# Other priorities for the early steps and fixed engines for normalising, copies and casts in an attention and MLP kernel

## The chip, the core and the metric

The kernel runs on one core of a Trainium2 chip. The metric is the device time of one execution in microseconds (us). TensorE is called PE, VectorE DVE, ScalarE ACT, GpSimd POOL, and SyncE SP, which issues all the transfers (DMA) of this kernel.

## What is computed

For each of 8 batches and 8 heads (576 positions of width 64) two softmax attentions are added: one over positions pooled by four, repeated four times, and a local one over the seven nearest positions. The sum, 4608 rows of 512, goes through a maxout MLP. Weights and products are held to float32 accuracy or better. The core of the reference:

```python
q_d = q.reshape(B, H, Sd, factor, D).mean(axis=3)       # k_d, v_d likewise
out_d = sm_attn(q_d, k_d, v_d)
out_up = np.repeat(out_d, factor, axis=2)
mask = np.abs(pos[:, None] - pos[None, :]) < factor      # seven neighbours
scores = np.where(mask, scale * np.matmul(q, k.transpose(0, 1, 3, 2)), -1e9)
attn_out = out_up + np.matmul(softmax(scores), v)        # x: 4608 x 512
h = np.maximum(np.maximum(x @ w1, x @ w2), x @ w3)       # 512 -> 768, three times
return h @ w_out                                         # 768 -> 512
```

## The kernel before

**Tiling.** The MLP runs in 9 blocks of 512 rows. A block j has 288 matmuls of 128x512 on PE: 6 column groups (`ft`) times 3 weights times 12 for the first layer (`mlp_in`), and 72 for the second (`mlp_out`). Twelve, not four, because each operand is a sum of two reduced-precision parts: `xhi`/`xlo` for the rows, `whi`/`wlo` for the weights, `hhi`/`hlo` for the hidden layer, `wohi`/`wolo` for the last weight; a product takes hi·hi, hi·lo and lo·hi. In PSUM `pm` has three banks: a group of 12 fills `ph_j_ft_i`; ACT copies the first to `t`, DVE takes the maximum with the second and the third (`t<-pm,t`), ACT casts to `hhi` (`hh_0r<-t`) and DVE subtracts for `hlo` (`hh_1r<-t,hh_0r`). A bank is free when its reader is done.

**Weights.** They arrive as words of 64 bit. For each of 6 column groups `weight_in(ft)` loads `rawin_ft`, and `weight_split` turns it into `whi`, `wlo`: ACT takes an absolute value, DVE runs two one-operand passes (TENSOR_SCALAR on `pvb`), two bit passes (SCALAR_TENSOR_TENSOR), ACT casts to `whi`, DVE subtracts for `wlo`. `weight_out` does the same with the last weight in six smaller pieces. In the trace `rawin_0` and `rawin_1` are `hh`, the later ones `wo`, the last weight's pieces `pvb`. Matmuls on `ft` need `whi` and `wlo` of that `ft`, and those on a row group c (0 to 3) need `xhi_j_c` and `xlo_j_c`.

**Attention.** Index n = 0..16 is half a block: four heads. The halves n = 0 to 3 (blocks 0 and 1) take a dense form in `dense(j, plan)`: steps listed in `PLAN`, each with a priority; `q` loads q and k, `qk` adds them up by four (`hp`, then `qkT`), `s0`/`s1` (`band_scores`) make local scores on PE, their maxima on DVE, exponentials (70 columns each) on ACT, the sum's reciprocal on DVE and the normalising product either as one DVE instruction or as eight on ACT; `v0`/`v1` (`band_values`) transpose them, copy them to SBUF (`ptb`), multiply with v and add the pooled part into `xb` (`t<-pm,od`, `x<-pa,od`); `sums`, `pv` do the pooled part (`pd`, `pt`, `od`). For n = 1 some of the tiles stand in the buffers of late weights, so `hp` reads `whi` and `wlo` in the trace. The halves n from 4 go through DRAM scratch and run beside the MLP of earlier blocks (`begin`, `attention`). `transposes(j, c)` casts to `xhi` and subtracts for `xlo`.

**What sets the order.** Every instruction is first recorded. `Recorder.place` then puts them in order, engine by engine, with a list of prices: it takes whatever can start first, and among those that can start, the lowest priority; an operation with several forms goes to the engine that would end first, plus a bias (`TO_ACT`, `MUL_BIAS`). Assumed delays are added between engines: `LAG`, and `CARE` for n from 4. `BEGIN` is the priority of the first steps of n = 4, `WLOAD`, `WMAKE`, `WOUT` those of the weights; `COLD_US` is how long PE is priced at half speed. The result is a fixed order on each engine (L492 issues it all), and each engine works strictly through its own list.

Of the kernel before, what the change touches and what calls it, by code (L numbers as in the profile page):

```python
# [32 lines left out]
VBUFS = 3  # L33
LAG = 200.0
TAGS = ('pm', 'pm', 'pa', 'pa')
WLOAD = (110.0, 165.0, 190.0, 320.0, 255.0, 350.0)
WMAKE = (150.0, 120.0, 110.0, 255.0, 285.0, 390.0)
WOUT = 300.0
PLAN = (
    (  # L40
        ("q", 0, -120.0),
        ("v", 0, -120.0),
        ("qk", 0, 0.0),
        ("s0", 0, -40.0),
        ("s1", 0, 100.0),
        ("tail", 0, 0.0),
        ("q", 1, 110.0),
        ("v", 1, 110.0),
        ("sums", 0, -40.0),
        ("vd", 0, 0.0),  # L50
        ("qk", 1, 70.0),
        ("s0", 1, 80.0),
        ("s1", 1, 100.0),
        ("tail", 1, 130.0),
        ("pv", 0, 180.0),
        ("v0", 0, -50.0),
        ("v1", 0, 60.0),
        ("sums", 1, 50.0),
        ("vd", 1, 220.0),
        ("pv", 1, 100.0),  # L60
        ("v0", 1, 70.0),
        ("v1", 1, 150.0),
    ),
    (
        ("q", 0, 200.0),
        ("v", 0, 200.0),
        ("qk", 0, 170.0),
        ("s0", 0, 320.0),
        ("s1", 0, 200.0),
        ("tail", 0, 270.0),  # L70
        ("sums", 0, 200.0),
        ("vd", 0, 200.0),
        ("pv", 0, 200.0),
        ("v0", 0, 200.0),
        ("v1", 0, 80.0),
        ("q", 1, 330.0),
        ("v", 1, 330.0),
        ("qk", 1, 420.0),
        ("s0", 1, 240.0),
        ("s1", 1, 360.0),  # L80
        ("tail", 1, 300.0),
        ("sums", 1, 240.0),
        ("vd", 1, 390.0),
        ("pv", 1, 300.0),
        ("v0", 1, 240.0),
        ("v1", 1, 300.0),
    ),
)
CARE = {'near': (2000.0, 2000.0, 1.1500000000000001), 'far': (3000.0, 2000.0, 1.2)}
NEAR = 8  # L90
# [99 lines left out]
class Recorder:  # L190
# [46 lines left out]
    def add(self, forms, bias={}):  # L237
# [4 lines left out]
        for method, args, kw in next(iter(forms.values())):  # L242
# [7 lines left out]
            ins += r  # L250
        o.prio = self.prio
        if "PE" in forms and o.prio >= 0.0:
# [257 lines left out]
def local_global_attention_maxout_kernel(ctx: ExitStack, tc: tile.TileContext, qk_d, qke_d, vw_d, vt_d, wi_d, wo_d, v, ident_d, mask_d, diag_d, band_d, out):  # L510
# [14 lines left out]
    def at(prio, lag=0.0, care=None):  # L525
# [18 lines left out]

    def copy(dst, src, engines=("ACT", "DVE"), bias={}):
        forms = {"ACT": [("copy", (dst, src), {})], "DVE": [("tensor_copy", (dst, src), {})]}
        return rec.add({e: forms[e] for e in engines}, bias)

# [144 lines left out]
    def pooled_scores(n):  # L693
# [24 lines left out]
        if n in DENSE:  # L718
# [6 lines left out]
            with together():  # L725
# [27 lines left out]
    def pooled_values(n):  # L753
# [123 lines left out]
    def band_scores(n, pr, tag):  # L877
# [19 lines left out]
        one = [("tensor_tensor", (), dict(out=sm, in0=sm, in1=z.unsqueeze(3).broadcast_to([P, 2, FAC, KWIN]), op=ALU.mult))]  # L897
        rec.add({"DVE": one, "ACT": muls}, TO_ACT)
        state[n]["sm", pr] = sm

    def band_values(n, pr, tag):
# [6 lines left out]
        for i in range(2):  # L908
# [48 lines left out]
    def transposes(j, c):  # L957
# [5 lines left out]
        else:  # L963
# [58 lines left out]
    def attention(n):  # L1022
# [92 lines left out]
```

## Time and profile before

| | |
|---|---|
| time before, median of 3 runs | 721.51 us (720.29 to 724.8) |
| the profiled execution: time | 722.12 us |
| its span, first to last instruction | 720.3 us |
| mean granted clock of PE | 0.985 |
| PE busy | 687.6 us (95%) |
| DVE busy | 525.8 us (73%) |
| ACT busy | 405.0 us (56%) |
| POOL busy | 204.3 us (28%) |

How it is read: a busy share is the time in which the engine ran instructions; idle time is named after whatever released the engine. All instructions have the line L492, so groups are told apart by engine, operation, tile names and shapes. Two full-speed matmuls of 128x512 start 0.2275 us apart; their own durations of 0.39 us overlap.

### The profile page before, as it was taken

The page shows a single profiled execution, that of the slowest core. Times are in us where ns is not written, and L with a number is a line of the kernel's source. Part 1 is how long each engine was busy: PE and PEld are TensorE (multiplying, and loading weights), DVE is VectorE, ACT ScalarE, POOL GpSimd, SP SyncE. Part 2 cuts the span into 40 slices and gives each one's busy share as a digit, 9 for nine tenths or more (in the row PEclk, how much of TensorE's full clock was granted, in tenths as well). Part 3 has the DMA queues.
Part 4 walks back from the last instruction along what each step waited for, and adds up shares of the span by engine and source line. Part 5 has one row for each costly group of instructions (what it writes and reads, how often), then busy time and mean ns, then how long its engine had stood idle before and what let it go on. Part 6 is the DMA issues. An engine that isn't in the chain of part 4 may idle for free.

```text
span 720.3 us, 13541 instructions
## 1 busy us (share of the span) xinstructions
PE 687.6 (95%) x4756; PEld 556.6 (77%) x4756; DVE 525.8 (73%) x928; ACT 405.0 (56%) x1437; POOL 204.3 (28%) x269
## 2 busy tenths in 40 slices
PE   3589999899999999999999999999999999999996
PEld 2467787688888888888887888888888788888885
DVE  5699998877878796879878987797868788531220
ACT  4988686473928482847475639273836577221111
POOL 0023200051615450445055307070515345000000
PEclk9959999999999999999999999999999999999999
DMA  9944234667486758493995574747475772210002
GB/s 275 416 173 154 88 124 149 160 157 153 121 189 186 124 131 179 110 201 75 235 208 114 102 204 120 181 92 210 115 189 109 177 133 70 55 59 30 0 1 58
DMA packets 190817, 101.35 MB, mean 141 GB/s; under 512 B 161454, under 2 KB 166605, under 8 KB 189981
## 3 DMA queue, kind: packets, MB, share of 16 engines
q1 hardware_dynamic: 190749, 100.49, 55.7%
q8 instruction: 37, 0.61, 0.4%
q14 instruction: 31, 0.25, 0.1%
HBM read 71.23 MB, written 29.23 MB: 139 GB/s over the span
## 4 chain that ended last, share of the span: by engine, by line
PE 85%; DVE 6%; ACT 4%; DMA 4%; issue 0%; SPq 0%; ACTq 0%; DVEq 0%
PE pm L492 78%; PE pa L492 7%; DVE pvb L492 1%; DMA pvb<-in_wo_dram 1%; ACT sm L492 1%; DMA wo<-in_wi_dram 1%; DVE wo L492 1%; DMA whi<-in_qk_dram 1%; DMA qk<-in_qk_dram 1%; ACT whi L492 1%; ACT pvb L492 1%; DVE t L492 1%; DVE hp L492 0%; DVE hh L492 0%; DVE wlo_0r L492 0%; ACT whi_0r L492 0%
## 5 line engine op out<-in xcount | busy, mean ns | idle before, releaser
L492 PE MATMUL pm<-xhi_0r,whi_0r 128*128 128x512 f32 x648 | 253.8, 392 | 0.9 <-ACT xhi_0r L492 0.9
L492 PE MATMUL pm<-xhi_0r,wlo_0r 128*128 128x512 f32 x648 | 253.2, 391 | 0.0
L492 PE MATMUL pm<-xlo_0r,whi_0r 128*128 128x512 f32 x648 | 253.2, 391 | 0.0
L492 POOL TENSOR_TENSOR pvb<-v,s 128x256 f32<-128x256 f32 x216 | 166.1, 801 | 171.2 <-DVE s L492 99.4
L492 ACT ACTIVATE pvb<-v,s 128x64 f32<-128x64 f32 x704 | 176.3, 343 | 26.0 <-DVE s L492 14.8
L492 PEld LDWEIGHTS pm<-xhi_0r,whi_0r 128*128 128x128 f32 x648 | 121.7, 188 | 27.9 <-ACT xhi_0r L492 1.3
L492 PEld LDWEIGHTS pm<-xhi_0r,wlo_0r 128*128 128x128 f32 x648 | 121.6, 188 | 25.8 <-issue 0.6
L492 PEld LDWEIGHTS pm<-xlo_0r,whi_0r 128*128 128x128 f32 x648 | 121.7, 188 | 25.6 <-issue 0.8
L492 DVE TENSOR_TENSOR t<-pm,t 128x512 f32<-128x512 f32 x108 | 73.8, 683 | 74.2 <-PE pm L492 69.1
L492 DVE TENSOR_TENSOR pvb<-pvb 128x768 f32<-128x768 f32 x112 | 109.6, 979 | 12.2 <-POOL pvb L492 7.6
L492 PE MATMUL pm<-wo_0r,hh_0r 128*128 128x512 f32 x216 | 84.4, 393 | 2.0 <-ACT wo_0r L492 2.0
L492 ACT CAST hh_0r<-t 128x512 fp32r<-128x512 f32 x54 | 33.5, 620 | 92.5 <-DVE t L492 92.2
L492 PE MATMUL pm<-wo_0r,hh_1r 128*128 128x512 f32 x216 | 84.5, 392 | 0.0
L492 PE MATMUL pm<-wo_1r,hh_0r 128*128 128x512 f32 x216 | 84.4, 391 | 0.0
L492 ACT CAST xhi_0r<-t 128x512 fp32r<-128x512 f32 x32 | 19.8, 620 | 61.6 <-DVE t L492 58.6
L492 PEld LDWEIGHTS pm<-wo_0r,hh_0r 128*128 128x128 f32 x216 | 40.5, 188 | 11.9 <-ACT wo_0r L492 2.5
L492 POOL TENSOR_TENSOR hv<-v 128x128 f32<-128x128 f32 (+1 forms) x14 | 12.8, 924 | 124.0 <-DMA v<-in_v_dram 111.8
L492 PEld LDWEIGHTS pm<-wo_1r,hh_0r 128*128 128x128 f32 x216 | 40.6, 188 | 8.8 <-issue 0.2
L492 PEld LDWEIGHTS pm<-wo_0r,hh_1r 128*128 128x128 f32 x216 | 40.5, 188 | 8.6 <-issue 0.2
L492 ACT COPY t<-pm 128x512 f32<-128x512 f32 x54 | 31.5, 584 | 27.7 <-PE pm L492 27.6
L492 DVE TENSOR_TENSOR hh_1r<-t,hh_0r 128x512 fp32r<-128x512 f32 x54 | 39.6, 733 | 9.9 <-ACT hh_0r L492 9.6
L492 ACT ACTIVATE pd<-pa,nz 128x144 f32<-128x144 f32 x90 | 33.1, 383 | 14.1 <-issue 11.1
(134 smaller groups left out, 711.2 us busy)
## 6 DMA issues: line engine op xcount, KB each, us to landing
v<-in_v_dram SPq DMA_DIRECT2D x55, 320.0 KB
qk<-in_qk_dram SPq DMA_DIRECT2D x30, 582.0 KB
out_dram<-y SPq DMA_DIRECT2D x36, 256.0 KB
scr<-sm SPq DMA_DIRECT2D x56, 140.0 KB
xd<-x SPq DMA_DIRECT2D x112, 64.0 KB
t<-xd SPq DMA_DIRECT2D x28, 256.0 KB
wo<-in_wi_dram SPq DMA_DIRECT2D x4, 1536.0 KB
pdd<-pd SPq DMA_DIRECT2D x48, 80.0 KB
```

What stands on the lines that cost most here:

```text
L492: getattr(self.engines[o.eng], method)(*map(real, args), **{k: real(x) for k, x in kw.items()})
```

## The change

Every instruction is still there and computes the same. Four things differ: the tables of priorities (`WLOAD`, `WMAKE`, `WOUT`, `PLAN`, `BEGIN`; a new `WHEN` for the halves 4 to 8, where it was 100·n); the assumed delays (`LAG`, `CARE`, `COLD_US`); `HOMES`, which fixes the engine for each normalising product (`norm`), copy of transposed scores (`band`, `pt`, `late`), cast (`hi`, `xhi`) and scaling of the pooled output (`od`) of the dense halves (A is ACT, D is DVE, - leaves it open); and `MUL_BIAS`, which keeps a product of `values` off DVE.

```diff
-LAG = 200.0
+LAG = 0.0
-WMAKE = (150.0, 120.0, 110.0, 255.0, 285.0, 390.0)
-WOUT = 300.0
+WMAKE = (2685.0, -90.0, 2725.0, 3485.0, 1910.0, -105.0)
+WOUT = -70.0
...
-        ("qk", 1, 70.0),
-        ("s0", 1, 80.0),
+        ("qk", 1, 4265.0),
+        ("s0", 1, -5285.0),
...
-CARE = {'near': (2000.0, 2000.0, 1.1500000000000001), 'far': (3000.0, 2000.0, 1.2)}
+CARE = {'near': (4500.0, 500.0, 1.2), 'far': (3500.0, 2500.0, 1.2)}
-MUL_BIAS = {'DVE': 3000.0}
-TO_ACT = {'DVE': 4000.0, 'POOL': 9000.0}
+MUL_BIAS = {'DVE': 7000.0}
+HOMES = {"norm": "DA-DD-DA", "band": "--AAA-AA--D-DA--", "hi": "-AD--A-DA-DD", "xhi": "-DAAA-AA", "od": "AA--", "pt": "-A-D", "late": "--A-"}
+WHEN = {4: 100, 5: 50, 6: 100, 7: 550, 8: 1100}
-COLD_US = 55.0
-BEGIN = 500.0
+COLD_US = 35.0
+BEGIN = 225.0
...
-        act.copy(hi, value)
+        copy(hi, value, homes("hi", k))
...
-            copy(pt[:, :, :P], pst1)
+            copy(pt[:, :, :P], pst1, homes("pt", n))
...
-        rec.add({"DVE": one, "ACT": muls}, TO_ACT)
+        forms = {"DVE": one, "ACT": muls}
+        rec.add({e: forms[e] for e in homes("norm", 2 * n + pr)})
...
-            copy(pt, ps, bias=TO_ACT)
+            copy(pt, ps, homes("band", 4 * n + 2 * pr + i))
...
-        act.copy(hi, xs)
+        copy(hi, xs, homes("xhi", 4 * j + c) if j < BANDED else ("ACT",))
```

What this moves is seen in the orders. Three places follow. In them a number behind a name is only the buffer's.

SP, at the start of the program, before; `whi_0_65` and `wlo_0_66` are q and k of n = 1, `hh_70` is `rawin_0`, `x` are windows of v:

```order
L492 DMA traw_104<-in_vt_dram 128x256
L492 DMA v_106<-in_v_dram 128x2x256
L492 DMA v_108<-in_v_dram 128x2x256
L492 DMA whi_0_65<-in_qk_dram 128x1164
L492 DMA x_119<-in_vw_dram 70x512
L492 DMA x_122<-in_vw_dram 70x512
L492 DMA x_144<-in_vw_dram 70x512
L492 DMA x_147<-in_vw_dram 70x512
L492 DMA wlo_0_66<-in_qk_dram 128x1164
L492 DMA whi_0_67<-in_vw_dram 70x512 x3
L492 DMA wlo_0_69<-in_vw_dram 70x512
L492 DMA wlo_0_69<-in_v_dram 128x2x256 x2
```

The same place of the change, where `hh_67` is `rawin_0` and `hh_69` is `rawin_1`:

```order
L493 DMA whi_0_65<-in_qk_dram 128x1164
L493 DMA wlo_0_66<-in_qk_dram 128x1164
L493 DMA traw_106<-in_vt_dram 128x256
L493 DMA hh_67<-in_wi_dram 128x3072
L493 DMA qk_117<-in_qk_dram 128x1164
L493 DMA v_120<-in_v_dram 128x2x256
L493 DMA v_142<-in_v_dram 128x2x256
L493 DMA v_144<-in_v_dram 128x2x256
L493 DMA hh_69<-in_wi_dram 128x3072
L493 DMA x_149<-in_vw_dram 70x512
```

q and k of n = 1 are issued 7th and 8th where they were 10th and 15th, `rawin_0` 10th where it was 22nd, and the windows of v behind `rawin_1`.

DVE, around the maxima of the fourth column group of block 0 (`t_0_3`), before; `wo_74` is `rawin_5`, `t_536` is `t_0_3`:

```order
L492 TENSOR_SCALAR pvb_97<-pvb_97 128x1536
L492 TENSOR_TENSOR t_536<-pm_126,t_536 128x512
L492 TENSOR_SCALAR nz_187<-nz_187 128x6
L492 RECIPROCAL rd_248<-nz_187 128x6
L492 TENSOR_TENSOR ptld_89<-pd_216,rd_248 128x2x32
L492 SCALAR_TENSOR_TENSOR wo_74<-wo_74,pvb_97 128x1536
L492 TENSOR_TENSOR t_536<-pm_124,t_536 128x512
L492 TENSOR_TENSOR ptld_89<-pd_216,diag_102 128x2x32
L492 SCALAR_TENSOR_TENSOR wo_74<-wo_74 128x1536
```

The same place of the change; `wo_75` is `rawin_5`, `t_496` is `t_0_3`:

```order
L493 TENSOR_SCALAR pvb_97<-pvb_97 128x1536
L493 SCALAR_TENSOR_TENSOR wo_75<-wo_75,pvb_97 128x1536
L493 TENSOR_SCALAR nz_181<-nz_181 128x6
L493 RECIPROCAL rd_230<-nz_181 128x6
L493 TENSOR_TENSOR ptld_89<-pd_211,rd_230 128x2x32
L493 SCALAR_TENSOR_TENSOR wo_75<-wo_75 128x1536
L493 TENSOR_TENSOR ptld_89<-pd_211,diag_102 128x2x32
L493 TENSOR_TENSOR t_496<-pm_122,t_496 128x512
L493 TENSOR_TENSOR t_496<-pm_124,t_496 128x512
```

Both maxima now stand behind both bit passes of `rawin_5`; before, each stood ahead of one.

PE, at the first matmuls of the MLP in the change; `pa_151<-pt_302,vd_525` is the pooled output of n = 1 (`pv`), `qk_117` the local scores of n = 2:

```order
L493 MATMUL pm_185<-xhi_0r,whi_0r 128x512
L493 MATMUL pm_185<-xlo_0r,whi_0r 128x512
L493 MATMUL pm_185<-xhi_0r,wlo_0r 128x512
L493 MATMUL pa_151<-pt_302,vd_525 64x144 x2
L493 MATMUL pa_153<-pt_302,vd_525 64x144 x2
L493 MATMUL pa_151<-ptt_93,vtail_0_565 64x144 x2
L493 MATMUL pa_153<-ptt_93,vtail_0_565 64x144 x2
L493 MATMUL pa_275<-x_0r 128x280
L493 MATMUL pa_280<-x_0r 128x280
L493 MATMUL pa_275<-qk_117 64x70
```

These two steps stand behind the first six matmuls of the MLP; before, both stood ahead of the first.

## Rows read from the trace of the kernel before

**Rows 1.** Busy time of each engine in stretches of the program: start:end, length, then for each engine busy us and number of instructions, then the granted clock of PE (1.00 is full speed), the share of the DMA engines and what they moved.

```profile
0.00:18.00 18.00, 6.22 (x93) 4.57 (x93) 9.67 (x25) 7.48 (x33) 0.20 (x4) 1.00 0.92 275
18.00:36.00 18.00, 9.91 (x124) 7.65 (x124) 11.57 (x29) 16.83 (x85) 0.17 (x1) 0.92 1.02 416
36.00:54.00 18.00, 14.98 (x169) 11.72 (x171) 17.80 (x24) 14.73 (x38) 3.97 (x5) 0.59 0.49 174
54.00:72.00 18.00, 17.14 (x156) 13.76 (x153) 17.42 (x31) 15.78 (x56) 5.93 (x2) 0.92 0.46 154
72.00:90.00 18.00, 17.42 (x181) 13.74 (x179) 17.31 (x25) 12.56 (x35) 5.35 (x4) 1.00 0.28 87
90.00:108.00 18.00, 18.00 (x133) 14.63 (x133) 17.16 (x31) 15.37 (x66) 0.82 (x2) 1.00 0.35 122
360.00:432.00 72.00, 72.00 (x496) 58.29 (x495) 61.63 (x113) 40.30 (x147) 27.77 (x39) 1.00 0.68 157
```

**Rows 2.** The timeline of PE: start, duration, instruction, and in brackets the idle time before it and its releaser. The first row is the first matmul of the MLP, 108.29 the first of the group that needs the bank of `ph_0_3_1`, 142.93 the first after the wait for the last weight, 150.69 the first of block 1, the last row the last matmul of the program.

```profile
58.19 0.50 PE L492 MATMUL pm<-xhi_0r,whi_0r 128*128 128x512 f32 x1
...
108.29 0.39 PE L492 MATMUL pm<-xhi_0r,whi_0r 128*128 128x512 f32 x1
...
142.93 0.96 PE L492 MATMUL pm<-wo_0r,hh_0r 128*128 128x512 f32 x3 [2.04 <-ACT wo_0r L492]
...
150.69 0.39 PE L492 MATMUL pm<-xhi_0r,whi_0r 128*128 128x512 f32 x1
...
713.57 0.39 PE L492 MATMUL pm<-wo_0r,hh_1r 128*128 128x512 f32 x1
```

**Rows 3.** The timeline of DVE from 0 to 33 us, only the rows with idle time of 0.8 us and more.

```profile
4.70 0.76 DVE L492 TENSOR_TENSOR hp<-qk 128x576 f32<-128x576 f32 x1 [3.48 <-DMA qk<-in_qk_dram]
...
12.65 0.76 DVE L492 TENSOR_TENSOR hp<-whi 128x576 f32<-128x576 f32 x1 [2.44 <-DMA whi<-in_qk_dram]
...
17.14 0.76 DVE L492 TENSOR_TENSOR hp<-wlo 128x576 f32<-128x576 f32 x1 [1.02 <-DMA wlo<-in_qk_dram]
...
19.48 0.17 DVE L492 TENSOR_SCALAR nz<-nz 128x6 f32<-128x6 f32 x1 [1.09 <-ACT pd L492]
...
22.12 0.17 DVE L492 TENSOR_SCALAR z<-z 128x8 f32<-128x8 f32 x1 [0.88 <-ACT sm L492]
...
27.66 0.17 DVE L492 TENSOR_SCALAR z<-z 128x8 f32<-128x8 f32 x1 [2.51 <-ACT whi L492]
...
31.74 0.96 DVE L492 TENSOR_SCALAR pvb<-pvb 128x1536 f32<-128x1536 f32 x1 [1.02 <-ACT pvb L492]
```

**Rows 4.** The chain that ended last, the piece from the issue of q and k of n = 1 to their landing (start, us, what).

```profile
6.14 6.50 DMA whi<-in_qk_dram
```

**Rows 5.** The timeline of ACT: two normalising products in their form of eight instructions, and the absolute value of `rawin_0`.

```profile
22.63 2.06 ACT L492 ACTIVATE sm<-sm,z 128x70 f32<-128x70 f32 x8 [0.54 <-DVE z L492]
...
28.16 2.06 ACT L492 ACTIVATE whi<-whi,z 128x70 f32<-128x70 f32 x8 [0.54 <-DVE z L492]
30.13 1.58 ACT L492 ACTIVATE pvb<-hh 128x1536 f32<-128x1536 f32 x1
```

**Rows 6.** Groups of instructions by operation and shape: count, busy us, mean ns of one, idle time before them. The first six are of DVE, the last of ACT.

```profile
L492 DVE SCALAR_TENSOR_TENSOR wo<-wo,pvb 128x1536 uint32<-128x1536 uint32 x4 | 7.0, 1755 | 0.1
L492 DVE TENSOR_TENSOR wlo_0r<-wo,whi_0r 128x1536 fp32r<-128x1536 f32 x4 | 7.0, 1752 | 0.1
...
L492 DVE TENSOR_SCALAR pvb<-pvb 128x1536 f32<-128x1536 f32 x6 | 5.8, 963 | 1.5 <-ACT pvb L492 1.5
...
L492 DVE TENSOR_SCALAR pvb<-pvb 128x512 f32<-128x512 f32 x6 | 2.5, 422 | 1.6 <-ACT pvb L492 1.6
...
L492 DVE COPY pt<-pa 128x512 f32<-128x512 f32 x3 | 2.1, 684 | 0.0
...
L492 DVE TENSOR_TENSOR pd<-pd,rd 128x512 f32<-128x512 f32 x2 | 1.4, 682 | 0.0
...
L492 ACT CAST whi_0r<-wo 128x1536 fp32r<-128x1536 f32 x4 | 6.5, 1627 | 4.5 <-DVE wo L492 4.5
```

**Rows 7.** The timeline of DVE: the last `xlo` of block 0, the two maxima of `t_0_3`, the second maximum of `t_0_5`, and the last subtraction for `wolo`.

```profile
64.52 0.69 DVE L492 TENSOR_TENSOR xlo_0r<-t,xhi_0r 128x512 fp32r<-128x512 f32 x1
...
102.97 0.68 DVE L492 TENSOR_TENSOR t<-pm,t 128x512 f32<-128x512 f32 x1
...
105.80 0.68 DVE L492 TENSOR_TENSOR t<-pm,t 128x512 f32<-128x512 f32 x1
...
131.99 0.68 DVE L492 TENSOR_TENSOR t<-pm,t 128x512 f32<-128x512 f32 x1
...
142.91 0.69 DVE L492 TENSOR_TENSOR wo_1r<-pvb,wo_0r 128x512 fp32r<-128x512 f32 x1 [0.63 <-ACT wo_0r L492]
```

**Rows 8.** The chain that ended last, the piece from the issue to the landing of the last piece of the last weight.

```profile
130.56 8.57 DMA pvb<-in_wo_dram
```

**Rows 9.** The timelines of DVE and PE where block 4 begins: the last `xlo` of the block, the block's first matmul, and its first matmul on row group 3, which reads that `xlo`'s `xhi`.

```profile
362.46 0.68 DVE L492 TENSOR_TENSOR xlo_0r<-t,xhi_0r 128x512 fp32r<-128x512 f32 x1
...
367.43 0.39 PE L492 MATMUL pm<-xhi_0r,whi_0r 128*128 128x512 f32 x1
...
369.47 0.39 PE L492 MATMUL pm<-xhi_0r,whi_0r 128*128 128x512 f32 x1
```

More of the change, by code (lines that the diff above doesn't have):

```diff
@@ L33 @@
 VBUFS = 3
-LAG = 200.0
+LAG = 0.0
 TAGS = ('pm', 'pm', 'pa', 'pa')
-WLOAD = (110.0, 165.0, 190.0, 320.0, 255.0, 350.0)
-WMAKE = (150.0, 120.0, 110.0, 255.0, 285.0, 390.0)
-WOUT = 300.0
+WLOAD = (110.0, 735.0, 1945.0, 2140.0, 25.0, -3535.0)
+WMAKE = (2685.0, -90.0, 2725.0, 3485.0, 1910.0, -105.0)
+WOUT = -70.0
 PLAN = (
     (
[L41 to L50, printed above, removed]
-        ("qk", 1, 70.0),
-        ("s0", 1, 80.0),
[L53 to L62, printed above, removed]
-    ),
-    (
[L65 to L86, printed above, removed]
@@ new lines @@
+        ("q", 0, -830.0),
+        ("v", 0, 1115.0),
+        ("qk", 0, 1890.0),
+        ("s0", 0, 1215.0),
+        ("s1", 0, 235.0),
+        ("tail", 0, 105.0),
+        ("q", 1, 85.0),
+        ("v", 1, 1665.0),
+        ("sums", 0, -150.0),
+        ("vd", 0, 240.0),
+        ("qk", 1, 4265.0),
+        ("s0", 1, -5285.0),
+        ("s1", 1, -1375.0),
+        ("tail", 1, 2010.0),
+        ("pv", 0, -465.0),
+        ("v0", 0, -5300.0),
+        ("v1", 0, -5.0),
+        ("sums", 1, -2350.0),
@@ new lines @@
+        ("vd", 1, 690.0),
+        ("pv", 1, 2585.0),
+        ("v0", 1, 940.0),
+        ("v1", 1, -580.0),
+    ),
+    (
+        ("q", 0, 155.0),
+        ("v", 0, 1190.0),
+        ("qk", 0, -1980.0),
+        ("s0", 0, 705.0),
+        ("s1", 0, -130.0),
+        ("tail", 0, 3630.0),
+        ("sums", 0, 275.0),
+        ("vd", 0, -480.0),
+        ("pv", 0, -910.0),
+        ("v0", 0, -1185.0),
+        ("v1", 0, -1575.0),
+        ("q", 1, -1725.0),
+        ("v", 1, 450.0),
+        ("qk", 1, 1520.0),
+        ("s0", 1, -1105.0),
+        ("s1", 1, 510.0),
+        ("tail", 1, -275.0),
+        ("sums", 1, -475.0),
+        ("vd", 1, 4215.0),
+        ("pv", 1, 885.0),
+        ("v0", 1, -980.0),
+        ("v1", 1, -895.0),
@@ L250, in add @@
             ins += r
-        o.prio = self.prio
+        o.prio = self.prio[next(iter(forms))] if isinstance(self.prio, dict) else self.prio
         if "PE" in forms and o.prio >= 0.0:
@@ L529, in at, with when @@
         rec.prio, rec.lag, rec.care = was
+    def when(n):
+        return WHEN.get(n, 100.0 * n)
     def care(n):
@@ L543, in either, with homes, copy, scaled @@
         return rec.add({e: [(method, (), kw)] for e in engines})
-    def copy(dst, src, engines=("ACT", "DVE"), bias={}):
+    def homes(what, k):
+        return {"A": ("ACT",), "D": ("DVE",), "-": ("ACT", "DVE")}[HOMES[what][k]]
+    def copy(dst, src, engines=("ACT", "DVE")):
         forms = {"ACT": [("copy", (dst, src), {})], "DVE": [("tensor_copy", (dst, src), {})]}
-        return rec.add({e: forms[e] for e in engines}, bias)
+        return rec.add({e: forms[e] for e in engines})
+    def scaled(dst, src, by, engines):
+        forms = {"ACT": [("mul", (dst, src, by), {})], "DVE": [("tensor_scalar_mul", (dst, src, by), {})]}
+        return rec.add({e: forms[e] for e in engines})
     def tt(out, in0, in1, op, engines=("DVE", "POOL")):
@@ L612, in load_constants, with weight_split @@
         sp.dma_start(diag, diag_d)
-    def weight_split(hi, lo, raw, a):
+    def weight_split(hi, lo, raw, a, k):
         low, high = raw[..., 0], raw[..., 1]
@@ L635, in weight_in @@
         with at(WMAKE[ft]):
-            weight_split(*(w.rearrange("p i c f -> p (i c f)") for w in (whi[ft], wlo[ft])), raw, a)
+            weight_split(*(w.rearrange("p i c f -> p (i c f)") for w in (whi[ft], wlo[ft])), raw, a, ft)
     def weight_out():
@@ L644, in weight_out @@
             sp.dma_start(raw.rearrange("p x t -> p (x t)"), wo_d[c * P : c * P + P].bitcast(U32))
-            weight_split(wohi[:, c], wolo[:, c], raw, part[:, 2 * DM :])
+            weight_split(wohi[:, c], wolo[:, c], raw, part[:, 2 * DM :], NFT + c)
     def halves(n, what, src, dst, engines=("DVE", "POOL")):
@@ L731, in pooled_scores @@
                 pe.matmul(pst2[:, 3 * P :], ptd, diag[:, HH + 2 :], start=True, stop=True, skip_group_check=True)
-            copy(pt[:, :, :P], pst1)
-            act.copy(pt[:, :, P:].rearrange("p (r i) x -> p i r x", i=2), pst2[:, : 2 * P].rearrange("p (i r x) -> p i r x", i=2, r=2)[..., QT - TAIL :])
-            act.copy(ptt, pst2[:, 2 * P :])
+            copy(pt[:, :, :P], pst1, homes("pt", n))
+            copy(pt[:, :, P:].rearrange("p (r i) x -> p i r x", i=2), pst2[:, : 2 * P].rearrange("p (i r x) -> p i r x", i=2, r=2)[..., QT - TAIL :], homes("late", n))
+            copy(ptt, pst2[:, 2 * P :], homes("late", n))
         else:
@@ L771, in pooled_values @@
             c = h0 // 2 + pr
-            act.mul(blk["od"][:, c], po[pr][:, :P], 0.25)
-            act.mul(odtail[:, c, j], po[pr][:, P:], 0.25)
+            scaled(blk["od"][:, c], po[pr][:, :P], 0.25, homes("od", n) if n in DENSE else ("ACT",))
+            scaled(odtail[:, c, j], po[pr][:, P:], 0.25, homes("od", n) if n in DENSE else ("ACT",))
     def window_scores(n, prs, tag="pa", masked=False):
@@ L1031, in attention @@
         if n < 2 * B + 1:
-            with at(100.0 * n + 100.0, LAG, care(n + 1)):
+            with at(when(n + 1), LAG, care(n + 1)):
                 begin(n + 1)
@@ L1060, in block @@
         for n in (2 * j, 2 * j + 1):
-            with at(100.0 * n, LAG, care(n)):
+            with at(when(n), LAG, care(n)):
                 attention(n)
```

## The prediction

> **What bounds the kernel now.** I read the busy time by stretches first [rows 1]. From 108 us on PE is all but full, and from the first matmul of block 1 at 150.69 to the last at 713.57 it is full: a stretch of 72 us has 72.00 us of busy PE [rows 1, 2]. The number and the size of its matmuls don't change. So the end moves only by what happens ahead of that point: the span is the time of the first matmul of block 1, plus a piece that the change can lengthen but hardly shorten.
>
> Ahead of it there are three stages. In the first, to 36 us, no engine is full and the DMA engines are (0.92 and 1.02) [rows 1]. DVE stands idle again and again, for transfers and for ACT [rows 3]. In the second, from 36 to 108 us, DVE is full: 17.80, 17.42, 17.31 and 17.16 us of each 18 [rows 1]. It splits weights and takes maxima; PE's first MLP matmul comes at 58.19. In the third, from 108 us, PE is full but for one wait of 2.04 us at 142.93 on the last piece of the last weight [rows 2].
>
> **The early idle time.** The seven waits of DVE add up to 3.48 + 2.44 + 1.02 + 1.09 + 0.88 + 2.51 + 1.02 = 12.4 us [rows 3]. The first stays, since the two first transfers stay. The other six, 9.0 us, are what the change attacks. q and k of n = 1 were issued at 6.14 and took 6.50 us [rows 4]; they now stand ahead of four windows of v and three other loads, so I put them at about 8.5 instead of 12.65 (some 2 us of earlier issue, the rest of the gain from the empty queue). Three of the four normalising products that stood between the exponentials on ACT at 2.06 us each [rows 5] now go to DVE, so the exponentials end earlier; DVE waited for those. `rawin_0` is issued 10th, and its absolute value, at 30.13 before [rows 5], need no longer wait behind exponentials; I walk it to about 18. Walking the lists of DVE, ACT and SP with the durations of the trace, about 0.8 us of the 9.0 stays and DVE has some 0.9 us less to do up to the last `xlo` of block 0, less about 0.9 of new small waits. That `xlo` stood at 64.52 [rows 7]; it comes to 64.52 − 8.2 = 56.3. The first MLP matmul comes to about 49. The two steps of n = 1 and n = 2 that PE had ahead of it (order of PE) now stand behind six matmuls, which is part of that gain on paper only.
>
> The granted clock in 36:54 was 0.59, and the first matmul took 0.50 us where later ones take 0.39 [rows 1, 2]. Matmuls that start at 49 may run at half speed, 0.46 us apart. They wait for DVE's `wlo` of the next column group anyway, until about 62, so I put this at nothing; without that cover 26 of them would cost 26 × 0.23 = 6 us.
>
> **What DVE gets in return.** From the last `xlo` of block 0 to the second maximum of `t_0_5` the new list of DVE has one cast of 128x1536 (`whi_2`), two normalising products, two copies of transposed scores and two casts of 128x512 more. By the nearest rows that is 0.96 + 2 × 0.68 + 2 × 0.68 + 2 × 0.42 = 4.5 us [rows 6]. The trace shows no cast on DVE. The nearest rows put it between 0.96 (one operand, 128x1536) and 1.75 us (two operands) [rows 6]; I take the one-operand value, since a cast reads one operand, and keep the other end: three casts at the upper end add 0.8 + 2 × 0.26 = 1.3 us. The Trainium skill, page "VectorE: DVE Perf Modes", section "The perf-mode tier table", gives one-operand operations on float32 in SBUF twice the rate of those on two tensors. By that rule it is the lower end, and the trace's 963 against 1752 ns agrees.
>
> ACT loses the same work at its own prices, 1.63 us for the large cast and 2.06 for a product [rows 5, 6]. After 54 us that is worth nothing, as ACT is busy 12.56 to 15.78 of 18 us [rows 1] and the idle waits behind it on DVE are early ones.
>
> **Where the lead goes.** The place is `t_0_3`. Before, its first maximum stood at 102.97 and the second at 105.80 [rows 7], each ahead of one bit pass of `rawin_5`. Now both stand behind both passes (order of DVE). Counted along both lists with the durations of the trace, DVE has 10.9 us more to do between the last `xlo` and that first maximum: 3.4 us of new work from the list above, 3.4 us for the two bit passes (1.75 each [rows 6], overlapping a little), and some 4 us for two `hp`/`qkT` pairs and small instructions of n = 3 and 4. Before, the stretch lasted 102.97 − 64.52 = 38.45 us [rows 7], of which DVE idled some 2 (its list there adds up to 36.5). So the maximum comes to 56.3 + 38.45 + 10.9 = 105.6, and ends at 106.3. It frees the bank that the group at 108.29 fills [rows 2]. PE, some 7 us ahead by then, has to stop for about 4 us, and goes on only 2.0 us earlier than before.
>
> From there to block 1 the trace has 150.69 − 108.29 = 42.4 us [rows 2], with the wait of 2.04 us in it. The last piece of the last weight was issued at 130.56 and took 8.57 us to land, behind other transfers [rows 8]. `WOUT` now has a lower priority number, so its pieces start earlier. DVE's list from `t_0_3` to the last `wolo` is 3.8 us shorter; before, it lasted 142.91 − 102.97 = 39.9 us [rows 7], so it ends at 105.6 + 36.1 = 141.7 at the latest, 1.2 us earlier. I take 1.5 of the 2.04 us as gained, between 0 and 2.04. The scores of n = 5, which PE did in this stretch, move behind the first matmuls of block 1: 1.2 us that only change place.
>
> Sum, against the profiled execution: −2.0 − 1.5 = −3.5 us at block 1, nothing after it. 722.12 − 3.5 = 718.6. The profiled execution lies 0.6 us above the median of the runs, 721.51, so the forecast is **718.0 us**.
>
> **After block 1.** The attention of n from 5 to 11 now stands 11 to 30 matmuls further down PE's list. Its last result is the `xlo` of a block. For block 4 it ended at 363.14 and the first matmul on that row group was at 369.47 [rows 9]: 6.3 us to spare. Thirty matmuls are 30 × 0.2275 = 6.8 us. I take nothing, since most groups are moved by 11 to 20 (2.5 to 4.6 us); the upper end is rival 3. `MUL_BIAS` keeps products of `values` off DVE, which is busy 61.63 of 72 us there [rows 1]; that relieves an engine with time to spare.
>
> **Rivals.**
> 1. The lead is kept. If DVE's idle time between 64 and 103 us vanishes as well, or the reordered small instructions cost less than I count, `t_0_3` comes near 101 and PE doesn't stop there. Then 7.5 us remain at block 1: 722.12 − 7.5 − 0.6 = 714.0. With all 8.2 and the 2.04 us it is 711.3. For it: PE itself has no more work than before, and DVE's list to the last `wolo` is only 6 us longer. Against it: the order of DVE at `t_0_3`.
> 2. DVE's new work eats everything. If the casts cost the upper end (1.3 us more), and the early waits keep 2 us more than I think, `t_0_3` comes at 108.9, and block 1 starts where it did: 722.12 − 0.6 = 721.5, and with 1 to 2 us more 723. For it: DVE is full from 36 to 108 us and gets 4.5 us more. The Trainium skill, page "Perfetto Trace Analysis", section "Identifying the Most-Contended Engine", says to improve the engine that is most occupied first; in this stretch that is DVE, which the change loads. By that rule this rival is the outcome, and the trace so far bears it out only in part, since DVE's early waits end on others.
> 3. Slower: the late attention. The place is the head of blocks 2 to 5, the point from which it decides is a delay of 6.3 us at the `xlo` [rows 9]. At 6.8 us and with the transfers through DRAM behind each other it would be late by some 2 us at four heads: 4 × 2 − 3.5 = 4.5, so 722.12 + 4.5 − 0.6 = 726. For it: 30 matmuls at the worst. Against it: the halves from 13 on are hardly moved, and most are within the spare time.
>
> **How the numbers follow.** Forecast (716 to 720) 0.45; rival 1 (711 to 716) 0.25; rival 2 (720 to 723.5) 0.20; rival 3 0.10. The range reaches from rival 1's best case to the upper end of rival 2, 711.0 to 723.5, and leaves out about 0.12. One per cent, about what a measurement of this kernel can tell from no change, is 7.2 us. Faster than 714.3 is about the whole of rival 1 and a little of the forecast's edge: 0.28. Slower than 728.7 is the far part of rival 3: 0.05. The rest, 0.67, is within 1%.
>
> **What would show it.** In the profile of the changed kernel: `hp<-whi` near 8.5 us; the absolute value of `rawin_0` near 18; the first MLP matmul near 49 and the last `xlo` of block 0 near 56; a stop of PE of about 4 us near 105, ended by DVE's `t<-pm,t`; block 1 starting near 147; and 72.00 us of busy PE in each 72 us after it. It is wrong if PE doesn't stop near 105 (rival 1), if the first matmul comes later than 53 (rival 2), or if PE idles at the head of blocks 2 to 5 (rival 3).

## The result and the profile after

The changed kernel takes 727.39 us in the median (20 runs), the kernel before 722.63 us (20 runs beside them): ratio 1.0063, 95% interval 1.0044 to 1.0081. One run of each kernel in a slower state (734.58 and 870.95 us) is left out of the ratio. The change is slower by 0.6%, where the forecast had 718.0 us, and it lies outside the range of 711.0 to 723.5. The profiled execution took 726.57 us, with a span of 724.8.

The busy time by stretches of the changed kernel; columns as in [rows 1].

```profile
18.00:36.00 18.00, 10.98 (x155) 7.91 (x147) 17.90 (x35) 15.90 (x65) 0.85 (x1) 0.78 0.99 295
...
144.00:216.00 72.00, 72.00 (x498) 58.54 (x497) 55.90 (x95) 42.01 (x151) 26.21 (x37) 1.00 0.70 151
216.00:288.00 72.00, 70.75 (x489) 56.90 (x488) 57.49 (x103) 41.65 (x156) 28.52 (x38) 1.00 0.72 155
288.00:360.00 72.00, 69.43 (x484) 56.06 (x484) 54.05 (x100) 43.87 (x162) 26.52 (x36) 1.00 0.68 140
...
504.00:576.00 72.00, 71.67 (x474) 57.79 (x473) 53.48 (x95) 41.32 (x158) 25.43 (x34) 1.00 0.68 140
576.00:648.00 72.00, 69.72 (x359) 57.31 (x358) 47.95 (x77) 40.55 (x134) 23.38 (x29) 0.98 0.38 95
```

The start is what was forecast: DVE, busy 11.57 of 18 us from 18 to 36 us before [rows 1], is now full there at 17.90. But PE, which before worked without a gap once block 1 had begun, now has gaps after 216 us, in four of the stretches (from 360 to 504 us each stretch of 72 us is full).

The timeline of PE in the changed kernel: the first MLP matmul, the stop near 103 us, the first matmul of block 1, the six longest waits after it, and the last matmul. The rows answer to [rows 2].

```profile
48.77 0.80 PE L493 MATMUL pm<-xhi_0r,whi_0r 128*128 128x512 f32 x1
...
102.80 0.50 PE L493 MATMUL pm<-xhi_0r,whi_0r 128*128 128x512 f32 x1 [1.55 <-ACT t L493]
...
144.76 0.39 PE L493 MATMUL pm<-xhi_0r,whi_0r 128*128 128x512 f32 x1
...
220.50 0.50 PE L493 MATMUL pm<-xhi_0r,whi_0r 128*128 128x512 f32 x1 [0.77 <-ACT y L493]
...
285.88 0.50 PE L493 MATMUL pm<-wo_1r,hh_0r 128*128 128x512 f32 x1 [0.49 <-ACT y L493]
...
294.58 0.50 PE L493 MATMUL pm<-xhi_0r,whi_0r 128*128 128x512 f32 x1 [0.92 <-ACT y L493]
...
322.61 0.71 PE L493 MATMUL pa<-pt,vd 128*64 128x144 f32 x8 [1.65 <-DMA pt<-pdd]
...
514.88 0.50 PE L493 MATMUL pm<-xhi_0r,whi_0r 128*128 128x512 f32 x1 [0.33 <-ACT y L493]
...
579.48 0.72 PE L493 MATMUL pa<-qk 64*64 64x70 f32 x32 [2.28 <-DMA qk<-in_qke_dram]
...
718.09 0.39 PE L493 MATMUL pm<-wo_1r,hh_1r 128*128 128x512 f32 x1
```

Block 1 begins at 144.76 instead of 150.69, 5.9 us earlier. Of these, 1.2 us only change place: the 64 small matmuls of the scores of n = 5 now stand behind that point. So the **lead** is 4.7 us. From there to the last matmul it took 713.57 − 150.69 = 562.9 us before [rows 2] and takes 718.09 − 144.76 = 573.3 now: 10.4 more, less the same 1.2, is a **loss** of 9.2 us. −4.7 + 9.2 = +4.5, and 726.57 − 722.12 = 4.45. The waits shown add up to 6.4 of the 9.2. PE's clock is the next piece, in the windows around the last wait (only PE: busy, granted clock, DMA share, GB/s):

```profile
579.00:581.00 2.00, 1.52 (x35) 0.88 0.10 41
581.00:583.00 2.00, 2.00 (x7) 0.50 0.35 133
583.00:585.00 2.00, 2.00 (x8) 0.77 0.47 147
```

The idle time of 2.28 us is followed by about 3.4 us at a granted clock of 0.50, 1.2 GHz: eight matmuls start 0.43 us apart instead of 0.2275, 1.6 us more. What is left of the 9.2, some 1.2 us, is in part the first matmul after each wait, 0.34 us to the next one; the remainder is not broken down.

**What the waits are.** `y` is the output of the second layer: ACT copies it out of its `pm` bank, and until then PE can't fill that bank. ACT's timeline in the changed kernel, ahead of the wait that ends at 220.50:

```profile
213.46 0.62 ACT L493 CAST xhi_0r<-t 128x512 fp32r<-128x512 f32 x1 [3.98 <-DVE t L493]
216.55 0.30 ACT L493 ACTIVATE s<-s 128x112 f32<-128x112 f32 x1 [2.47 <-DVE s L493]
216.75 0.37 ACT L493 ACTIVATE pd<-pa,nz 128x144 f32<-128x144 f32 x1
...
218.90 1.07 ACT L493 ACTIVATE pvb<-v,s 128x64 f32<-128x64 f32 x4
219.85 1.08 ACT L493 COPY y<-pm 128x512 f32<-128x512 f32 x2
```

The same place in the kernel before:

```profile
214.60 0.62 ACT L492 CAST xhi_0r<-t 128x512 fp32r<-128x512 f32 x1 [6.68 <-DVE t L492]
215.13 0.58 ACT L492 COPY y<-pm 128x512 f32<-128x512 f32 x1
216.19 0.62 ACT L492 CAST xhi_0r<-t 128x512 fp32r<-128x512 f32 x1 [0.48 <-DVE t L492]
216.71 0.58 ACT L492 COPY y<-pm 128x512 f32<-128x512 f32 x1
```

Before, both copies stood right behind the casts. Now they stand behind the exponential of `s`, whose scores come through DRAM, then six exponentials of `pd` and four products. ACT sits idle 2.47 us in front of that exponential. The first of the two outputs is finished only as this idle time ends: its last matmul starts at 215.94 and takes 0.39 us. So what its copy then stands behind is 3.3 us of work (216.55 to 219.85) that the wait had pushed back. At the wait that ends at 285.88 a finished output does stand behind an idle ACT. The rows of PE (the last matmul of each of the two outputs) and of ACT:

```profile
215.94 0.39 PE L493 MATMUL pm<-wo_1r,hh_1r 128*128 128x512 f32 x1
...
280.92 0.39 PE L493 MATMUL pm<-wo_1r,hh_1r 128*128 128x512 f32 x1
...
284.72 0.62 ACT L493 CAST xhi_0r<-t 128x512 fp32r<-128x512 f32 x1 [6.00 <-DVE t L493]
285.25 0.58 ACT L493 COPY y<-pm 128x512 f32<-128x512 f32 x1
```

The output is ready at 281.31, and its copy starts at 285.25, behind a cast for whose rows ACT idles 6.00 us. ACT is busy only 54% of the span; its list, not its load, is late.

The other two long waits are loads that SP issues late. The chain that ended last in the changed kernel, from SP's loads to PE:

```profile
568.56 3.43 SPq L493
...
572.92 6.52 DMA qk<-in_qke_dram
...
579.48 0.72 PE pa L493 x32
580.20 138.29 PE pm L493 x602
```

SP's timeline at the issue of that load, in the kernel before:

```profile
544.23 0.33 SPq L492 DMA_DIRECT2D qk<-in_qke_dram  x1
```

The load of q and k of n = 17 is issued at 572.92 instead of 544.23, behind loads and stores that hold SP. From its landing PE works through to the end, so in this execution the chain of the whole program hangs on this load. The load of `pt` for n = 8 is the same case: 318.28 instead of 308.48.

### The profile page after: what moved, and what is told of

It reads as the page before. It is cut to its first block, busy times and chain, and to the rows that moved or that the text cites. A ratio compares the mean times of both kernels' runs of the same rounds, so it can differ in the third digit from the quotient of the medians.

```text
span 724.8 us, 13489 instructions
## 1 busy us (share of the span) xinstructions
PE 689.8 (95%) x4756; PEld 555.4 (77%) x4756; DVE 531.4 (73%) x941; ACT 392.7 (54%) x1403; POOL 195.2 (27%) x268
## 5 line engine op out<-in xcount | busy, mean ns | idle before, releaser
L493 POOL TENSOR_TENSOR pvb<-v,s 128x256 f32<-128x256 f32 x211 | 161.7, 800 | 189.3 <-DVE s L493 97.4
L493 ACT ACTIVATE pvb<-v,s 128x64 f32<-128x64 f32 x724 | 181.1, 342 | 26.2 <-DVE s L493 19.9
L493 PE MATMUL pm<-wo_1r,hh_1r 128*128 128x512 f32 x216 | 85.2, 394 | 0.0
L493 PEld LDWEIGHTS pm<-wo_1r,hh_1r 128*128 128x128 f32 x216 | 40.9, 189 | 9.0 <-issue 0.6
L493 DVE TENSOR_TENSOR t<-t,od 128x512 f32<-128x512 f32 x24 | 16.3, 688 | 42.4 <-DMA t<-xd 31.7
L493 ACT COPY y<-pm 128x512 f32<-128x512 f32 (+1 forms) x44 | 25.3, 587 | 40.5 <-PE pm L493 39.8
```

The costliest lines, as they stand in the source:

```text
L493: getattr(self.engines[o.eng], method)(*map(real, args), **{k: real(x) for k, x in kw.items()})
```

## Experiments

**Is it the lists behind the start?** In the first four, one late load is moved (e1), then several late places (e2), and the delays alone are swapped (e3, e4). Each ratio is against the kernel before, timed beside the run on the same chip.

e1 and e2 are the change with instructions of SP's and ACT's lists moved; each line names the instruction, which one of that name, and behind which other it now stands. First e1, then e2:

```diff
+    (('SP', 'qk_17_1'), 0, ('PE', 'sb_16_0_0')),
```

```diff
+    (('SP', 'qk_17_1'), 0, ('PE', 'sb_16_0_0')),
...
+    (('SP', 'pt_8'), 0, ('SP', 's_9')),
+    (('ACT', 'pvb'), 39, ('ACT', 'y_1_3')),
+    (('ACT', 'xhi_3_2'), 0, ('ACT', 'y_2_0')),
...
```

> The changed kernel with one load moved up in SP's list: the second load of q and k of n = 17, which PE waited 2.28 us for near 580, now stands right behind what frees its buffer. Theory A (the lead of the early stage is real, and is lost at single places where an instruction stands too late in a list that is worked in order): the gap of 3.96 us becomes 1.45 and the stretch of PE at half speed after it goes, 2.5 + 1.7 = 4.2 us less than the changed kernel, about 723, level with the kernel before. Theory B (the later attention can't go faster than before, whatever stands where, so a repaired place hands its wait to the next): less than 1 us.

> As e1_qk17, and the other places too: the loads of the pooled weights of n = 8 on SP (PE waited 1.65 us near 322) ahead of four transfers, and five operations of ACT (three groups of products, two casts) moved behind the copies of y that PE waited for near 220, 285, 294 and 514. Theory A: 4.2 + 1.7 + 3.1 = 9 us less than the changed kernel, about 718.5, and ahead of the kernel before by 4 us. Theory B: 4 us less at most, with new waits on the same tiles later.

Measured: e1 1.0085 (1.0054 to 1.0116), e2 1.0079 (1.0050 to 1.0108), no better than the change. The moved load no longer stopped PE, but PE's timeline of e1 has others just behind it:

```profile
586.42 0.49 PE L519 MATMUL pm<-wo_1r,hh_0r 128*128 128x512 f32 x1 [1.52 <-ACT y L519]
...
595.49 0.50 PE L519 MATMUL pm<-xhi_0r,whi_0r 128*128 128x512 f32 x1 [1.27 <-ACT y L519]
```

In e2 one wait of 2.49 us for ACT's `y` stands at 584.00, behind an `xhi` cast that waited 9.42 us for its rows. So a single late place doesn't carry the loss: take one away, and PE waits at the next, as theory B had it.

e3, the changed kernel with the old delays and priorities of the halves (the diff); e4, the kernel before with the new ones and the new `MUL_BIAS`:

```diff
-CARE = {'near': (4500.0, 500.0, 1.2), 'far': (3500.0, 2500.0, 1.2)}
+CARE = {'near': (2000.0, 2000.0, 1.1500000000000001), 'far': (3000.0, 2000.0, 1.2)}
-WHEN = {4: 100, 5: 50, 6: 100, 7: 550, 8: 1100}
+WHEN = {}
```

> The changed kernel with the assumed delays CARE and the priorities WHEN of the halves from 4 on as before; all else is changed. If these two tables put the instructions in the wrong places (theory A, with the tables as the cause): 718 to 720. If any order after the faster start loses as much (theory B), or another part of the change is the cause: 725 to 728.

> The kernel before with CARE, WHEN and MUL_BIAS of the change, and nothing else of it. If the tables are the cause: 5 to 9 us slower than before, 727 to 731. If the cause lies in the early part: 722 to 724.

Measured: e3 1.0089 (1.0065 to 1.0114), e4 1.0191 (1.0155 to 1.0227), slower than either theory had it for e4. Neither half of the change is good with the other half of the kernel before. e3 has already lost most of its lead at block 1, with waits of 1.42 and 2.09 us for the last weight. After block 1 PE waits 7.1 us in e4 (6.4 in the changed kernel), but in other places: all of it for `xhi` and `xlo` early in a block, the longest here:

```profile
601.08 0.96 PE L493 MATMUL pm<-xhi_0r,whi_0r 128*128 128x512 f32 x3 [2.79 <-ACT xhi_0r L493]
```

So the loss doesn't go with the old tables, and the new ones by themselves bring another one: what a table does depends on the order that comes out of it. The next runs fix the lists.

**Splices.** e5 takes the change's lists up to the first matmul of block 1 and those of before from there; e6 the reverse; e7 is the change again; e8 is the change with twelve copies `y` moved ahead of the waiting steps on ACT, and six loads moved forward on SP. e5, e6 and e8 issue a written list in place of the planned order:

```diff
-        out = self.place()
+        out = self.listed()
```

ACT's list in e8 against the change's, at the first of the six places:

```diff
+y_1_2 y_1_3
 s_6 pd x6 pvb x4
-y_1_2 y_1_3
```

> The order of the change on all engines up to the first matmul of block 1, and from there on the order of the kernel before, for all that is not yet done. Theory A2 (the start of the change is worth 4 to 5 us, and its later lists lose 9): 4 to 5 us less than the kernel before, a ratio near 0.994. Theory B (the later attention can't follow a start that is 5 us earlier, in whatever order): level with the kernel before, a ratio of 0.998 to 1.003.

> The reverse: the order of the kernel before up to the first matmul of block 1, and the order of the change from there on. Theory A2: the later lists lose their 9 us without the start's gain, a ratio near 1.012. Theory B: no lead, so nothing to lose: 1.000 to 1.003.

> The changed kernel itself, as the measure for the others on this chip: 5 to 6 us slower than the kernel before (1.006 to 1.009), with waits of PE for copies of y at the heads of blocks whose length differs from one execution to the next.

> The changed kernel with twelve copies of y moved ahead, in ACT's list, of the softmax, cast and product instructions that wait for transfers (near 218, 285, 293, 514, 583 and 594), and six loads moved up in SP's list (q and k of n = 17, the pooled weights of n = 8, the last two loads of xs of block 7). PE's and DVE's lists are untouched. Theory A2 with ACT's and SP's lists as the place: PE's waits for y after block 1 go, 5 to 8 us less than the changed kernel, level with the kernel before or 3 us ahead. If those waits only move on (to the cast, or to the scores): less than 3 us.

Measured: e5 720.27 us, 0.9961 (0.9937 to 0.9985); e6 733.00, 1.0135 (1.0091 to 1.0179); e7 726.96, 1.0057 (1.0029 to 1.0084); e8 723.59, 1.0022 (0.9998 to 1.0045). The start is worth something, the later lists lose it and more. e5's gain of 2.3 us lies between the two theories; e6 is what theory A2 had. In e6 PE's waits behind block 1 are the change's, for `y`, for `pt` of n = 8 and for q and k of n = 17, though its block 1 starts only 0.4 us earlier than before:

```profile
226.79 0.80 PE L746 MATMUL pm<-xhi_0r,whi_0r 128*128 128x512 f32 x1 [2.69 <-ACT y L746]
...
330.21 0.71 PE L746 MATMUL pa<-pt,vd 128*64 128x144 f32 x8 [2.15 <-DMA pt<-pdd]
...
587.03 0.72 PE L746 MATMUL pa<-qk 64*64 64x70 f32 x32 [2.67 <-DMA qk<-in_qke_dram]
```

So these waits need no early start. e8 gets back 3.4 of the change's 4.4 us (e7, beside it) with the order of copies and loads alone, less than the 5 to 8 expected; how much of it is the copies' and how much the loads' was not tried. ACT's timeline of e8 at the place shown above:

```profile
214.07 0.62 ACT L747 CAST xhi_0r<-t 128x512 fp32r<-128x512 f32 x1 [3.59 <-DVE t L747]
217.41 1.27 ACT L747 COPY y<-pm 128x512 f32<-128x512 f32 x2 [2.72 <-PE pm L747]
218.57 0.30 ACT L747 ACTIVATE s<-s 128x112 f32<-128x112 f32 x1
```

The copies now wait for PE, not PE for them; PE's wait at 220.50 is gone from its timeline.

**What the early start is made of.** e9 to e11 change e5 in one place each, beside e5 itself again (e12). e9 returns three normalising products to ACT (the diff leaves their engine open, and its written list puts them on ACT); e10 gives SP the early sequence of loads of before; e11 moves two loads and four additions of DVE (`hp` and `qkT` of n = 5) behind the last weight.

```diff
-HOMES = {"norm": "DA-DD-DA", "band": "--AAA-AA--D-DA--", "hi": "-AD--A-DA-DD", "xhi": "-DAAA-AA", "od": "AA--", "pt": "-A-D", "late": "--A-"}
+HOMES = {"norm": "-A----DA", "band": "--AAA-AA--D-DA--", "hi": "-AD--A-DA-DD", "xhi": "-DAAA-AA", "od": "AA--", "pt": "-A-D", "late": "--A-"}
```

SP's list in e10 (first pair of lines) and in e11, against e5's:

```diff
-qk0_1 qk1_1 traw_0 rawin_0 qk_2_0 v_0_0 v_0_2
+traw_0 v_0_0 v_0_2 qk0_1 vwin_0 x4 qk1_1
...
-qk_5_1 qk_6_0 pvb (sixth)
+pvb (sixth) qk_5_1 qk_6_0
```

> The splice (the change's lists up to the first matmul of block 1, then the lists of before), with the three early normalising products that the change gave to DVE put back on ACT (one of sm_0, two of sms_1), at the same places of the lists. Theory F, the forecast's term: the waits of 1.09, 0.88 and 2.51 us [rows 3] came from ACT, so they return, 4.5 us, less the 2 us of DVE work saved: the first MLP matmul comes about 2.5 us later than the splice's, 51 to 52 us, block 1 starts 1 to 2.5 us later, and the time is 1 to 3 us above the splice's. Rival L: the early start comes from the order of the loads alone and ACT has room: first matmul within 0.7 us of the splice's, time within 1 us of it.

> The splice with SP's early loads in the sequence of before (first head's traw, v and vwin loads again ahead of rawin_0 to rawin_2), nothing else changed. Theory F: the waits of 2.44 and 1.02 us for loads [rows 3] return, and rawin_0's first pass waits as in before: first MLP matmul 3 to 7 us later than the splice's (52 to 56 us) and block 1 2 to 4 us later; the time 2 to 5 us above the splice's, at or above the time of before. Rival: the sequence of the loads is worth nothing, since the other engines' lists decide: first matmul within 0.7 us of the splice's, time within 1 us.

> The splice with what stands ahead of the last weight of block 0 moved behind it: on SP two qk loads (n of 5 and 6) behind the sixth of the pvb loads, on DVE two pairs of hp products of n of 5 behind the last wolo. Theory W: the wait of 2.27 us near 135 is the weight's rounding standing late in DVE's list; it shrinks below 1 us, the 3.4 us at half clock that follow it go, and the time falls 1 to 4 us below the splice's. Rival B: the rounding waits for its transfer through the two stage buffers, which DVE's list does not decide: the wait stays at 1.5 us or more, and the time within 1 us of the splice's.

> The splice itself once more, the measure for the runs beside it on this chip: first MLP matmul near 49 us, block 1 near 149, one wait of about 2 us near 135 for the last weight, and a time 1.5 to 4 us below the kernel before.

Measured, beside 722.12 us of e12: e9 726.21, e10 739.80, e11 723.13. DVE's timeline and PE's first MLP matmul in e9:

```profile
17.54 0.17 DVE L747 TENSOR_SCALAR nz<-nz 128x6 f32<-128x6 f32 x1 [2.97 <-ACT pd L747]
...
40.08 0.17 DVE L747 TENSOR_SCALAR nz<-nz 128x6 f32<-128x6 f32 x1 [2.14 <-ACT wlo L747]
...
53.11 0.80 PE L747 MATMUL pm<-xhi_0r,whi_0r 128*128 128x512 f32 x1
```

The same in e10:

```profile
11.78 0.76 DVE L747 TENSOR_TENSOR hp<-whi 128x576 f32<-128x576 f32 x1 [4.25 <-DMA whi<-in_qk_dram]
...
33.54 0.76 DVE L747 TENSOR_TENSOR hp<-qk 128x576 f32<-128x576 f32 x1 [11.41 <-DMA qk<-in_qk_dram]
...
65.75 0.80 PE L747 MATMUL pm<-xhi_0r,whi_0r 128*128 128x512 f32 x1
```

e9: the waits for ACT are back, 5.1 us in two places, the first matmul comes 4.4 us later than in e12 (48.72), and the time is 4.1 us longer: theory F's mechanism, at nearly twice the size; the 2 us saved on DVE don't show in it. e10: the direction of theory F, but some four times the size. The lists of the other engines now ask for q and k of n = 2 early, and DVE waits 11.41 us for them: the first matmul is later than in the kernel before (58.19 [rows 2]). With the old sequence of loads the new lists are worse than the old ones: here the two only work as a pair.

e11: rival B. PE's wait for the last weight is 2.02 us at 139.55. DVE sat idle 3.54 us for ACT at the last piece, and ACT 6.97 us for its transfer, in ACT's timeline of e11:

```profile
135.91 0.66 ACT L747 ACTIVATE pvb<-pvb 128x512 f32<-128x512 f32 x1 [6.97 <-DMA pvb<-in_wo_dram]
```

The transfer was issued at 128.27, no earlier than in e5 (127.73) although two loads ahead of it were moved away. Neither DVE's list nor these two loads decide this wait. How long it is changes between executions of the same lists, 2.27 us in e5 and 0.48 in e12, so one execution can't price it.

**All of them side by side.** Lead: how much earlier than at 150.69 the first matmul of block 1 starts. Loss: by how much the piece from there to the last matmul is longer than 562.9 us. Where the scores of n = 5 stand behind that point (the lists of the change from the start: after, e7, e1, e2, e3, e8) 1.2 us are taken off both. One profiled execution each; the ratio is that of the timed runs. A profiled execution can lie some us from its kernel's median: e7's took 730.46 us (median 726.96), e8's 722.51 (723.59), so the 7.5 us between their losses are 3.4 in the timed runs.

| kernel | lists to block 1 | lists behind | lead us | loss us | ratio |
|---|---|---|---|---|---|
| after | change | change | 4.7 | 9.2 | 1.0063 |
| e7 | change | change | 3.3 | 11.6 | 1.0057 |
| e1 | change | change, 1 load moved | 3.4 | 13.1 | 1.0085 |
| e2 | change | change, 9 moved | 3.5 | 10.7 | 1.0079 |
| e8 | change | change, 18 moved | 3.7 | 4.1 | 1.0022 |
| e3 | change, old delays | same | 0.8 | 9.0 | 1.0089 |
| e4 | before, new delays | same | −3.7 | 10.2 | 1.0191 |
| e6 | before | change | 0.4 | 12.4 | 1.0135 |
| e5 | change | before | 2.0 | 1.3 | 0.9961 |
| e12 | change | before | 4.6 | 5.8 | 0.9972 |
| e11 | change, weight forward | before | 3.2 | 3.1 | 0.9991 |
| e9 | change, norm on ACT | before | −0.1 | 2.5 | 1.0026 |
| e10 | change, old loads | before | −14.1 | 1.4 | 1.0217 |

Every kernel whose lists behind block 1 were made with any of the new numbers loses 9.0 to 13.1 us there, whatever its lead, but for e8, which has copies and loads moved; those with the lists of before lose 1.3 to 5.8. e5 and e12 are one kernel. It is faster than the kernel before in both measurements, by 0.39 and 0.28%, and than the change beside it (e7).

## Why the prediction was wrong, step by step

**The early idle time: right.** [rows 3] had six waits of 9.0 us, and one of 0.97 us is left. The rows of the changed kernel that the prediction named, on DVE (the first row is `hp` of n = 1, forecast near 8.5; the second the last `xlo` of block 0, forecast 56.3):

```profile
8.46 0.76 DVE L493 TENSOR_TENSOR hp<-whi 128x576 f32<-128x576 f32 x1 [0.97 <-DMA whi<-in_qk_dram]
...
56.40 0.68 DVE L493 TENSOR_TENSOR xlo_0r<-t,xhi_0r 128x512 fp32r<-128x512 f32 x1
```

The absolute value of `rawin_0` starts at 17.91 (forecast 18), the first MLP matmul at 48.77 (49). e9 shows the switch of engines as a cause, e10 that the loads are needed with it.

**What DVE gets in return: right.** The casts, which the trace of before did not show on DVE, take the lower end of their bounds:

```profile
L493 DVE CAST wo_1r<-pvb 128x512 fp32r<-128x512 f32 x4 | 1.7, 424 | 0.1
L493 DVE CAST whi_0r<-wo 128x1536 fp32r<-128x1536 f32 x1 | 1.0, 978 | 0.0
```

978 and 424 ns stand beside 963 and 422 of the one-operand passes [rows 6]. The tier rule of the Trainium skill, page "VectorE: DVE Perf Modes", section "The perf-mode tier table", agrees. Rival 2, DVE's new work eating the lead, did not come: 4.7 us were left at block 1. The Trainium skill, page "Perfetto Trace Analysis", section "Identifying the Most-Contended Engine", spoke for it; this trace does not bear it out: the time went later, to waits on ACT (54% busy) and on loads.

**The stop near 105: size and releaser wrong, the sum near by luck.** The maxima of `t_0_3` start at 104.83 (forecast 105.6), but PE's stop is 1.55 us, not 4, and it is ended by ACT's copy `t` at 102.14, behind six exponentials: the group that started at 108.29 [rows 2] now fills the bank that this copy frees, and starts at 102.80, 5.5 us earlier and not 2.0. The wait for the last weight shrank from 2.04 us to 0.7 in two pieces (forecast −1.5), but behind the stop PE has some 1.7 us more of small attention matmuls, which the prediction didn't count. So block 1 starts 4.7 us to the good instead of 3.5. The seven profiled executions with these lists up to block 1 (after, e7, e1, e2, e8, e5, e12) lie between 2.0 and 4.7 us, around the forecast, but two terms were off in opposite directions.

**The step that failed is "After block 1 ... I take nothing"**, and with it "nothing after it" in the sum: it measured +9.2 us, which with the 1.2 us gained ahead of block 1 is the whole miss of the profiled execution (726.57 against 718.6). The working followed one dependence, the `xlo` of a block, and how far PE's list moved. Two things were left out. The later attention's instructions moved on ACT against the copies `y`, and a copy behind an instruction that waits for DRAM, or behind the work that such a wait has pushed back, holds a bank of PE; ACT's low load says nothing of this. And SP's loads moved behind others: the forecast walked SP's list only at the start. e6 shows that it costs as much without any early start, e8 that moving copies and loads takes most of it away (3.4 of 4.4 us in the timed runs). The rest of the loss stays open.

**Rival 3** had the sign and nearly the time (726), for another reason: PE idled near the heads of blocks 2 and 3 (220.50 and 294.58), but for ACT's `y`, and the longest waits were two loads. That the time fits is luck. No wait for an `xlo` was among them: measured as in [rows 9], the spare time fell from 6.9 to 3.2 us at block 2 and from 9.4 to 2.8 at block 5, but ran out at no block. The 6.3 us of block 4 weren't the least either: block 7 had 2.4 us before. Waits of rival 3's kind came in e4. **Rival 1**'s kept lead came in part: 4.7 us at block 1 in the change, not 7.5; with the lists of before behind it (e5) it gave 2.3 us in the time (e12 2.0). Its chance was also put too high: faster than 714.3 us got 0.28, though rival 1 as a whole, 711 to 716, had 0.25 and the forecast's band begins at 716.

**Left open:** why a lead isn't kept even with the lists of before. In e5 2.0 us of lead lost 1.3, in e12 4.6 lost 5.8, and e10, 14 us late, lost only 1.4; e9 with no lead lost 2.5, so it is no simple rule. That PE, when early, meets transfers whose times don't move with it fits e12 (0.65 us twice for `pt`, 1.84 and 0.98 us for ACT's `y`), but no run tried it.

## What to carry to other kernels

When an order changes, look at every engine's list behind the place where the gain is, not only at the engine that is full: for each instruction that frees a buffer of the bounding engine, ask what now stands ahead of it, and whether that waits for a transfer or was pushed back by such a wait. A lightly loaded engine that works in order (ACT at 54%, SP) can stop a full one. An order made from assumed delays can have a good start and a bad rest; splicing the lists of two kernels at a common point, both ways, shows which part is which.

## What the runs showed of the hardware

PE, at a granted clock of 1.00 (2.4 GHz) in the stretches around, fell to a granted clock of 0.50 (1.2 GHz) for about 3.4 us soon after the wait of 2.28 us in the changed kernel (1.0 us after its end) and after that of 2.27 us in e5 (1.5 us), here e5's windows of PE:

```profile
135.00:137.00 2.00, 1.68 (x7) 0.95 0.57 29
137.00:139.00 2.00, 2.00 (x7) 0.50 0.00 0
139.00:141.00 2.00, 2.00 (x8) 0.70 0.00 0
```

In e7 such a fall came after waits of 1.92 and 1.94 us and none after one of 2.15; in e11 none after 2.02. So the length of the wait alone doesn't tell whether the clock falls, and where it falls a short wait can cost some 1.7 times its length: (2.28 + 1.6) / 2.28. And the same lists wait differently from run to run: at the last weight e5 2.27 us, e12 0.48; the runs of the changed kernel lie between 723.08 and 732.22 us.
